# Tensor-product message passing on a graph: a bucket's 17 tiles cut into parts of 4, 6 and 7 instead of 5, 6 and 6

## The chip, the core and the metric

The kernel runs on one core of one Trainium2 chip. The metric is the device time of one execution in microseconds (us); lower is better. The core has five engines with an instruction queue each: PE (TensorE, the matmuls; PEld is its weight load), DVE (VectorE), ACT (ScalarE), POOL (GpSimd) and SP (SyncE). In this kernel SP issues the plain DMAs and POOL the indirect ones, in which a list of row numbers says what is read or written.

## What is computed

A graph has N = 10000 nodes and E = 640000 edges. Each node carries 64 channels of 4 components, 256 floats. Each edge has a source, a destination, four values Y and four features.

```python
R = silu(edge_feat @ w_rad)                      # (E, 64)
xs = x[src]                                      # (E, 64, 4), gathered
tp = jnp.einsum('eci,ef,ifo->eco', xs, Y, cg)    # (E, 64, 4)
msg = R[:, :, None] * tp
agg = segment_sum(msg.reshape(-1, 256), dst, N).reshape(N, 64, 4)
return jnp.einsum('ncm,cd->ndm', agg, w_mix)     # (N, 64, 4)
```

Sources and destinations are drawn at random. So each edge needs a row of x from an arbitrary place, and its message goes to an arbitrary node.

## The kernel before, in words

**The sort.** Edges are handled in tiles of 128, one edge to a partition. The kernel first sorts them by destination into buckets of NB = 32 nodes, of which there are 313; 18 buckets make a group, and there are 18 groups (the last one is short, with 7 buckets). The sort has two passes, and both work through chunks of 12 tiles. Pass 1 (`pass1`) packs an edge into 10 words and sends it to its group; pass 2 (`pass2`) reads a group back and sends its edges to their buckets. For one chunk `route` computes where each edge goes. VectorE spreads the words over slots (`spread`, lines 637 to 645: a mask, then X) and makes a part of the one-hot rows (`rows`, lines 654 to 660), ScalarE makes the others, PE permutes (`move`), ScalarE evicts (`evict`), and POOL stores the rows with one indirect DMA (`store`, line 687; grp is the table of pass 1, bkt that of pass 2). Each batch of chunks also needs `tables` of counts and offsets, a chain of small steps over PE, ScalarE and VectorE.

**The parts.** The edges are cut into three parts by SPLIT (line 39). Each entry has a share of the edges and the number of tiles that a bucket gets from this part, 5, 6 and 6 of BT = 17. Lines 103 to 106 turn the shares into ranges of tiles, rounded to 24. Line 111 gives the tiles of a group in each part: its mean number of edges with a margin, rounded up. A bucket that gets more edges from a part than it has room for passes the rest on to the later parts. In the last part two neighbouring buckets share one tile, so units there have 6 and 5 tiles in turn.

**The messages.** One unit is one bucket in one part (`messages`), so there are 3 x 313 = 939 units. `gather` fetches the unit's rows of x, one indirect DMA of POOL for each tile (line 1030), LG = 5 units ahead, into LG + 2 buffers named xg. `turn` transposes the features of the unit's tiles on PE, in two blocks of three tiles each, which overlap where a unit has five. `turned` copies them to SBUF on ScalarE, `radial` multiplies them with the radial weights on PE, and `silu` runs on ScalarE in place. `spots` builds the matrix S (destination and Y) on VectorE (lines 1066 and 1069; lines 1073 to 1077 for the shared tile), `products` multiplies xg with the radial scalars on VectorE (line 1083), and `sums` adds the tiles up in PSUM with two matmuls for each (line 1098). In the first two parts `evict` copies the sums out on ScalarE (line 1127) into the tile Gp, which has two buffers, and SP stores it to DRAM (line 1128). In the last part `fetch` reads the two stored sums back (line 1108, tile "old", three buffers), `evict` adds them on VectorE (lines 1123 and 1125), and `mix` applies cg and w_mix for four buckets at a time.

**The order of the work.** The first part's pass 1 runs alone, with the clearing of the tables woven in (lines 1549 to 1560). Then `groups` runs all else interleaved, in quarter steps of a unit. While the messages of one part run, pass 2 of the same part is worked off, each group in time for its messages, and pass 1 of the next part is spread evenly (`later`, lines 1189 to 1194, with due times and costs by the number of chunks). The messages of the last part have only its pass 2 beside them. The order of the instructions of PE, VectorE and ScalarE is exactly as the program writes it; on POOL and SP a scheduler orders them ahead of the run. Every engine works through its own queue in order.

Constants that VectorE reads often lie in a PSUM tile, dv: `v64` (the numbers 0 to 63), `i32` (its first 32 numbers), the work area `eq`, which has UT tiles' room, and a mask area, `vmsk`. `i128`, in SBUF, has the numbers 0 to 127.

Of the kernel before, what the change touches and what calls it, by code (L numbers as in the profile page):

```python
# [18 lines left out]
F = mybir.dt.float32  # L19
BF = mybir.dt.bfloat16  # L20
I32 = mybir.dt.int32
OP = mybir.AluOpType
AF = mybir.ActivationFunctionType
AX = mybir.AxisListType

P = 128
# [7 lines left out]
NB = 32  # L34
GN = B * NB
BT = 17
PT = 2 * BT - 1
UT = 6
SPLIT = ((0.32, 5), (0.37, 6), (0.31, 6))
LG = 5  # L40
LI = 8
HEAVY = 4
BIG = 16384.0
# [4 lines left out]
KR = 108  # L48
# [31 lines left out]
class Kernel:  # L80
    def __init__(self, ctx, tc, x, src, dst, Y, ef, w_rad, cg, w_mix, out):
# [16 lines left out]
        N, E, T, r = self.N, self.E, 12, 14  # L98
        assert N <= 127 << 7 and BT == sum(u for _, u in SPLIT) and B % 2 == 0 and HB % 2 == 0
        self.NG = (N + GN - 1) // GN  # L100
        assert self.NG <= B
        self.part, cut = [], 0
        for i, (share, _) in enumerate(SPLIT):
            end = cut + round(self.NT * share / (2 * T)) * 2 * T if i + 1 < len(SPLIT) else self.NT
            self.part.append((cut, end))
            cut = end
        self.gt = []
        for a, z in self.part:
# [8 lines left out]
        self.gbase = [[(k * NG + g) * self.p1.stride + self.p1.cap - self.gt[k][g] * P // r for g in range(NG)]  # L117
                      for k in range(len(SPLIT))]
        self.NBK = (N + NB - 1) // NB
# [6 lines left out]
        self.btile = [0]  # L126
        for _, u in SPLIT:
            self.btile.append(self.btile[-1] + u)

        self.p1.ovf = len(SPLIT) * NG * self.p1.stride  # L130
        self.p2.ovf = self.pairs * self.p2.stride
# [23 lines left out]
    def consts(self):  # L155
        nc, c = self.nc, self.cst
# [17 lines left out]
        self.i128 = iota("i128", [[1, P]])  # L174

        self.dv = self.ps.tile([P, 512], F, name="dv", tag="dv", bufs=1)
        self.v64 = self.dv[:, 0:P // 2]
        nc.vector.tensor_copy(self.v64, self.i128[:, :P // 2])
        self.i32 = self.dv[:, 0:NB]
        self.eq = self.dv[:, P:P + UT * NB].rearrange("p (t n) -> p t n", n=NB)  # L180
        self.vmsk = self.dv[:, P + UT * NB:]

        ib = self.ph.tile([P, P], BF, name="ib", bufs=1)
        nc.vector.tensor_copy(ib, self.i128)
        nc.vector.tensor_copy(self.dv[:, P // 2:P].bitcast(I32), ib.bitcast(I32))
        self.vb = self.dv[:, P // 2:P].bitcast(BF)

        self.sh = c.tile([P, 8], I32, name="sh")
        for a in range(2):
# [389 lines left out]
    def route(self, ps, quad, nt, table):  # L579
# [4 lines left out]
        nc, wk, tc, T, Q = self.nc, self.ph, self.tc, ps.T, 2  # L584
# [48 lines left out]
        def spread(c):  # L633
            _, slot, _ = MS[c // (2 * Q)]
            o, a = c % (2 * Q) * T, c % Q * T
            m = min(T, nt - c * T)
            msk = self.vmsk[:, :m * ps.r].rearrange("p (t s) -> p t s", s=ps.r)
            nc.vector.tensor_tensor(msk, self.v64[:, :ps.r].unsqueeze(1).to_broadcast([P, m, ps.r]),
                                    slot[:, o:o + m].unsqueeze(2).to_broadcast([P, m, ps.r]), op=OP.is_equal)
            X = self.ph.tile([P, self.xw], F, name="X", bufs=3)[:, :T * ps.rw].rearrange("p (t w) -> p t w", t=T)  # L640
            nc.vector.tensor_tensor(  # L641
                X[:, :m, :].rearrange("p t (s w) -> p t s w", w=W),
                msk.unsqueeze(3).to_broadcast([P, m, ps.r, W]),
                QD[c // Q][1][:, a:a + m, :].unsqueeze(2).to_broadcast([P, m, ps.r, W]), op=OP.mult)
            XO[c] = X
# [290 lines left out]
    def messages(self):  # L936

        nc, ph = self.nc, self.ph
        units = [((k, g), j) for k, g in self.segs for j in range(self.nb(g))]
        MT, FIN = max(u for _, u in SPLIT), len(SPLIT) - 1  # L940
        n = len(units)
        IDX, XG, PRE, ST_, RT, SS, VS, GP, GS, OLD, E9, ER, SX, VX = ({} for _ in range(14))
# [7 lines left out]
        def place(g, j):  # L950

            n = SPLIT[g[0]][1]
            if g[0] < FIN:
                return j * n, n
            return j // 2 * (2 * n - 1) + j % 2 * n, n - j % 2

        def tiles(k):
            return place(*units[k])

        def shared(k):  # L960

            g, j = units[k]
            return g[0] == FIN and j % 2 == 0 and j + 1 < self.nb(g[1])
# [60 lines left out]
        def gather(k):  # L1024
            g, j = units[k]
            si, (t0, ut) = IDX[g][0], tiles(k)
            xg = XG[k] = ph.tile([P, UT, 256], F, name="xg", bufs=LG + 2)
            for t in range(ut):
# [5 lines left out]
        def turn(k):  # L1034
            g, j = units[k]
            t0, ut = tiles(k)


            pre = PRE[k] = self.ps.tile([P, 512], F, name="pre", tag="pre", bufs=2)
            e = E9[g, j // HB].rearrange("p t h q k -> p (t h q k)")  # L1040
            b = t0 - place(g, j - j % HB)[0]
            for h, t in ((0, b), (1, b + ut - 3)):
                nc.tensor.matmul(pre[:KR, 256 + 128 * h:384 + 128 * h], e[:, 36 * t:36 * t + KR],  # L1043
                                 self.identb, start=True, stop=True)

        def turned(k):
            sT = ST_[k] = ph.tile([P, 2, P], BF, name="sT")
            nc.scalar.activation(sT[:KR].rearrange("p h e -> p (h e)"), PRE[k][:KR, 256:512], AF.Copy)  # L1048

        def radial(k):  # L1050
            ut = tiles(k)[1]
            R = RT[k] = PRE.pop(k)[:, :ut * 64]
            sT = ST_.pop(k)

            nc.tensor.matmul(R[:, :192], sT[:KR, 0], self.wr[:KR], start=True, stop=True)
            nc.tensor.matmul(R[:, 192:], sT[:KR, 1], self.wr[:KR, (6 - ut) * 64:], start=True, stop=True)  # L1056

        def silu(k):
            nc.scalar.activation(RT[k], RT[k], AF.Silu)  # L1059
# [1 line left out]
        def spots(k):  # L1061
            g, j = units[k]
            t0, ut = tiles(k)
            pb = self.pay[g][:, t0:t0 + ut]
            dl = IDX[g][1][:, t0:t0 + ut]
            nc.vector.tensor_tensor(self.eq[:, :ut], self.i32.unsqueeze(1).to_broadcast([P, ut, NB]),
                                    dl.unsqueeze(2).to_broadcast([P, ut, NB]), op=OP.is_equal)
            S = SS[k] = ph.tile([P, UT, NB, 4], F, name="S")
            nc.vector.tensor_tensor(S[:, :ut], self.eq[:, :ut].unsqueeze(3).to_broadcast([P, ut, NB, 4]),  # L1069
                                    pb[:, :, 1:5].unsqueeze(2).to_broadcast([P, ut, NB, 4]), op=OP.mult)  # L1070
            if shared(k):

                eq = ph.tile([P, NB], F, name="eqx", bufs=1)
                nc.vector.tensor_scalar(eq, self.v64[:, NB:2 * NB], dl[:, ut - 1:ut], None, op0=OP.is_equal)
                S = SX[k + 1] = ph.tile([P, NB, 4], F, name="Sx")
                nc.vector.tensor_tensor(S, eq.unsqueeze(2).to_broadcast([P, NB, 4]),
                                        pb[:, ut - 1, 1:5].unsqueeze(1).to_broadcast([P, NB, 4]), op=OP.mult)
# [25 lines left out]
        def fetch(k):  # L1103

            g, j = units[k]
            if g[0] == FIN:
                OLD[g, j] = ph.tile([P, FIN, 2, 4, NB], F, name="old", bufs=3)
                nc.sync.dma_start(OLD[g, j].rearrange("p a h f n -> p a (h f n)"),
                                  self.sums[g[1] * B + j].rearrange("a p q -> p a q"))

        def evict(k):
            g, j = units[k]
            final = g[0] == FIN
            if not final:
                to = ph.tile([P, 2, 4, NB], F, name="Gp")
            else:
                if j % 4 == 0:
                    GS[g, j // 4] = ph.tile([P, 2, 4, 4, NB], F, name="Gs")
                to = GS[g, j // 4][:, :, :, j % 4, :]
            G = GP.pop((g, j)).rearrange("p h n f -> p h f n")  # L1120
            if final:
                old = OLD.pop((g, j))
                nc.vector.tensor_tensor(to, old[:, 0], G, op=OP.add)
                for a in range(1, FIN):
                    nc.vector.tensor_tensor(to, to, old[:, a], op=OP.add)  # L1125
            else:
                nc.scalar.activation(to, G, AF.Copy)  # L1127
                nc.sync.dma_start(self.sums[g[1] * B + j, g[0]], to.rearrange("p h f n -> p (h f n)"))
# [18 lines left out]
        def mixed(k, po):  # L1147
# [6 lines left out]

        quarters = (((index, LI), (gather, LG), (fetch, 1), (turn, 2), (sums, 0), (silu, 1), (piece(0), 5), (piece(1), 4),
                     (piece(2), 3)), ((turned, 2), (spots, 1)),
# [85 lines left out]
    def mark(self):  # L1242
        for s in self.marks:
            self.nc.tensor.wait_ge(s, 1)

    def chunks(self, part):
        lo, hi = self.part[part]
        return (hi - lo + self.p1.T - 1) // self.p1.T
# [351 lines left out]
```

## Time and profile before

| | |
|---|---|
| median of 3 runs | 8426.91 us (8418.68 to 8428.72) |
| the profiled execution | 8430.4 us, of which the span from the first to the last instruction is 8428.6 us |
| mean granted TensorE clock | 0.855 |
| busy share of the span: DVE, PE, POOL, PEld, ACT | 85%, 71%, 70%, 59%, 55% |
| gathers of x by POOL (line 1030) | 5165, mean 957 ns, 4940.6 us in all |
| stores of the sort by POOL (line 687) | 417 to grp and 489 to bkt, mean 1008 ns |
| products (line 1083) | 939, mean 1615 ns |
| moved by DMA | 1051.54 MB |

How to read it: the shares are means over stages that differ much, so each stage is looked at by itself below. In the list of groups a line gives the program's line, the engine, the operation, output and inputs by the program's names, shapes and count, then the busy time in us and the mean of one in ns, and then the idle time of the engine just before them and what ended it. "issue" as that reason means that the engine waited for nothing that the profile shows. A lower-case q behind an engine's name is its sequencer, which issues and waits. The list of windows gives for each stretch its length, and for each engine its busy time and its number of instructions.

### The profile page before, as it was taken

To read this page: it belongs to the slowest core of one execution; us is meant where nothing else is said; L and a number is where in the kernel's file an instruction comes from. 1 tells how busy PE (TensorE), PEld (TensorE's weight loads), DVE (VectorE), ACT (ScalarE), POOL (GpSimd) and SP (SyncE) were. 2 spreads that over 40 slices of the span, in tenths; PEclk is the share of its full clock that TensorE was granted. 3 is DMA by queue.
4 is the path that set the end of the run, shared out by engine and by line. 5 is a ranking of instruction groups with operands and counts; after the bars stand their busy time and mean duration, and the time that the engine had idled before them with its cause. 6 is when DMAs were issued, how large, how long until landed. Compare 5 with 4: busy or idle time off the path is not lost. (4 is left out here: it accounts for less than half of the span.)

```text
span 8428.6 us, 133579 instructions
## 1 busy us (share of the span) xinstructions
PE 5985.1 (71%) x41164; PEld 4943.4 (59%) x41164; DVE 7181.2 (85%) x14990; ACT 4614.3 (55%) x12740; POOL 5881.9 (70%) x6113
## 2 busy tenths in 40 slices
PE   5666776777767767776676676766677777778776
PEld 3334655656555656565565565555566666666666
DVE  8988999999999889988898898867787888878775
ACT  5876666666666746655565565653443443434321
POOL 1226676777767767777777777777777777777776
PEclk8977888888888879888888888887898989888888
DMA  5313343443434434444444444444455555555543
GB/s 185 112 59 96 113 117 107 118 116 112 118 110 120 119 112 129 121 122 123 120 122 124 120 119 125 116 120 121 133 147 145 145 146 145 146 148 143 146 139 114
DMA packets 691501, 1051.54 MB, mean 125 GB/s; under 512 B 268789, under 2 KB 499107, under 8 KB 690792
## 3 DMA queue, kind: packets, MB, share of 16 engines
q0 software_dynamic: 285888, 732.64, 30.5%
q1 hardware_dynamic: 402312, 301.08, 12.1%
q10 hardware_dynamic: 2592, 9.19, 0.3%
q8 instruction: 345, 5.65, 0.3%
q14 instruction: 364, 2.98, 0.1%
HBM read 841.86 MB, written 215.89 MB: 125 GB/s over the span
## 5 line engine op out<-in xcount | busy, mean ns | idle before, releaser
L1030 POOL DMA_INDIRECT xg<-in_x_dram,sidx x5165 | 4940.6, 957 | 1750.4 <-issue 1345.0
L1098 PE MATMUL G<-S,xg 128*128 128x128 f32 x20660 | 2989.8, 310 | 158.2 <-ACT Gp L1127 129.4
L1098 PEld LDWEIGHTS G<-S,xg 128*128 128x128 f32 x20660 | 2837.7, 222 | 202.2 <-ACT Gp L1127 153.3
L675 PE MATMUL pr<-X,oh 128*128 128x300 bf16 (+1 forms) x10573 | 1668.3, 312 | 548.5 <-DVE oh L657 411.4
L1083 DVE TENSOR_TENSOR xg<-xg,pre 128x1536 f32<-128x1536 f32 (+1 forms) x939 | 1516.4, 1615 | 540.3 <-DMA xg<-in_x_dram,sidx 303.3
L665 ACT ACTIVATE sq<-i,rowf 128x128 f32<-128x128 f32 x6132 | 1882.1, 391 | 11.2 <-DVE rowf L626 7.3
L641 DVE TENSOR_TENSOR X<-dv,Wt 128x1800 f32<-128x1800 f32 (+4 forms) x906 | 1741.6, 1922 | 62.1 <-PE pr L675 10.4
L675 PEld LDWEIGHTS <-oh 128*128 128x128 bf16 x10573 | 1080.1, 105 | 983.1 <-DVE oh L657 483.7
L666 ACT ACTIVATE oh<-sq,ones 128x1024 bf16<-128x1024 f32 (+3 forms) x906 | 967.1, 1067 | 27.1
L1069 DVE TENSOR_TENSOR S<-dv,pay 128x768 f32<-128x768 f32 (+1 forms) x939 | 836.7, 891 | 87.3 <-PE G L1098 29.8
L1043 PE MATMUL pre<-identb,e 128*108 128x128 bf16 x1878 | 291.2, 241 | 867.5 <-DVE xg L1083 866.6
L1043 PEld LDWEIGHTS <-e 128*108 128x108 bf16 x1878 | 236.8, 140 | 1041.1 <-issue 792.3
L1059 ACT ACTIVATE pre<-pre 128x384 f32<-128x384 f32 (+1 forms) x939 | 426.6, 454 | 716.3 <-PE pre L1056 551.0
L687 POOL DMA_INDIRECT grp<-rt,idx x417 | 420.2, 1008 | 529.0 <-ACT rt L683 196.9
L1127 ACT ACTIVATE Gp<-G 128x256 f32<-128x256 f32 x626 | 238.6, 381 | 892.0 <-PE G L1098 647.3
L687 POOL DMA_INDIRECT bkt<-rt,idx x489 | 492.7, 1008 | 224.7 <-issue 112.4
L1048 ACT ACTIVATE sT<-pre 108x256 bf16<-108x256 f32 x939 | 353.2, 376 | 527.1 <-PE pre L1043 525.2
L1143 PE MATMUL po<-wf,Gs 128*128 128x256 f32 (+2 forms) x1392 | 390.8, 443 | 184.6 <-DVE Gs L1125 184.6
L683 ACT ACTIVATE rt<-pr 128x300 bf16<-128x300 f32 (+1 forms) x906 | 358.7, 396 | 278.6 <-PE pr L678 118.5
L1143 PEld LDWEIGHTS po<-wf,Gs 128*128 128x128 f32 (+2 forms) x1392 | 282.5, 209 | 278.1 <-DVE Gs L1125 181.7
L657 DVE TENSOR_TENSOR oh<-dv,pair 128x640 bf16<-128x640 bf16 (+2 forms) x869 | 420.6, 488 | 0.3
L609 ACT ACTIVATE pc<-pp 128x432 f32<-128x432 f32 (+3 forms) x471 | 236.3, 502 | 295.5 <-DVE pos L618 227.5
(286 smaller groups left out, 6086.1 us busy)
## 6 DMA issues: line engine op xcount, KB each, us to landing
xg<-in_x_dram,sidx POOLq DMA_INDIRECT x5165
sums<-Gp SPq DMA_DIRECT2D x626, 128.0 KB
old<-sums SPq DMA_DIRECT2D x313, 256.0 KB
bkt<-z SPq DMA_DIRECT2D x26, 990.0 KB
pay<-bkt SPq DMA_DIRECT2D x68, 225.0 KB
grp<-z SPq DMA_DIRECT2D x17, 590.0 KB
Wt<-grp SPq DMA_DIRECT2D x17, 590.0 KB
ye<-in_Y_dram SPq DMA_DIRECT2D x103, 96.0 KB
```

What stands on the lines that cost most here:

```text
L641: nc.vector.tensor_tensor(X[:, :m, :].rearrange("p t (s w) -> p t s w", w=W), msk.unsqueeze(3).to_broadcast([P, m, ps.r, W]), QD[c // Q][1 ...
L665: nc.scalar.activation(sq[:, u, :], self.i128, AF.Square, bias=to, scale=-1.0)
L666: nc.scalar.activation(oh[:, v:v + len(at), :], sq[:, :len(at), :], AF.Relu, bias=self.ones[:, 0:1], scale=-2.0)
L675: nc.tensor.matmul(pr[:, :2 * ps.rw], oh[:, u, :], X[:, u, :].bitcast(BF), start=(u == 0), stop=(not on and u == m - 1))
L687: st = nc.gpsimd.indirect_dma_start(out=ps.dst, out_offset=bass.IndirectOffsetOnAxis(ap=idx[:, i:i + 1], axis=0), in_=RT.pop(c), in_offset ...
L1030: nc.gpsimd.indirect_dma_start(out=xg[:, t, :], out_offset=None, in_=self.x, in_offset=bass.IndirectOffsetOnAxis(ap=si[:, u:u + 1], axis=0))
L1043: nc.tensor.matmul(pre[:KR, 256 + 128 * h:384 + 128 * h], e[:, 36 * t:36 * t + KR], self.identb, start=True, stop=True)
L1059: nc.scalar.activation(RT[k], RT[k], AF.Silu)
L1069: nc.vector.tensor_tensor(S[:, :ut], self.eq[:, :ut].unsqueeze(3).to_broadcast([P, ut, NB, 4]), pb[:, :, 1:5].unsqueeze(2).to_broadcast([P ...
L1083: nc.vector.tensor_tensor(V, V, R.unsqueeze(3).to_broadcast([P, ut, 64, 4]), op=OP.mult)
L1098: nc.tensor.matmul(G[:, h].rearrange("p n f -> p (n f)"), v[:, 32 * h:32 * h + 32, :].rearrange("p c i -> p (c i)"), s.rearrange("p n f -> ...
L1143: nc.tensor.matmul(po[:nn, :256], Gs[:, h, f].rearrange("p b n -> p (b n)")[:, :nn], self.wf[:, h, f, :], start=(h + f == 0), stop=(h + f ...
```

## The change

The shares become 0.258, 0.375 and 0.367, with 4, 6 and 7 tiles of a bucket; the sum stays 17. Units of the last part now have 7 and 6 tiles in turn. The transposes of a unit go in as many blocks of three tiles as it takes: two for 4, 5 or 6 tiles, three for 7, with the last block drawn back so that it ends with the unit's last tile. `turned` copies as many blocks as there are, and `radial` runs one matmul for each block, on the columns that no earlier block has covered.

Units have up to seven tiles (UT), so the buffers of xg and S grow. In return gathers go four units ahead (LG), with six xg buffers instead of seven; Gp has one buffer instead of two, and "old" has two (the pool's own number) instead of three. The PSUM tile dv is laid out anew: the 64 numbers of `v64` become the 32 of `i32`, and the shared tile's comparison (line 1074) takes its numbers 32 to 63 from `i128`.

```diff
-UT = 6
-SPLIT = ((0.32, 5), (0.37, 6), (0.31, 6))
-LG = 5
+UT = 7
+SPLIT = ((0.258, 4), (0.375, 6), (0.367, 7))
+LG = 4
...
-            msk ... self.v64[:, :ps.r] ...
+            msk ... self.i32[:, :ps.r] ...
...
-            for h, t in ((0, b), (1, b + ut - 3)):
-                nc.tensor.matmul(pre[:KR, 256 + 128 * h:384 + 128 * h], e[:, 36 * t:36 * t + KR],
+            for h, t in enumerate(self.thirds(ut)):
+                t += b
+                nc.tensor.matmul(pre[:KR, P + P * h:2 * P + P * h], e[:, 36 * t:36 * t + KR],
                                  self.identb, start=True, stop=True)
...
-            sT = ST_[k] = ph.tile([P, 2, P], BF, name="sT")
-            nc.scalar.activation(sT[:KR].rearrange("p h e -> p (h e)"), PRE[k][:KR, 256:512], AF.Copy)
+            sT = ST_[k] = ph.tile([P, 3, P], BF, name="sT")
+            n = P * len(self.thirds(tiles(k)[1]))
+            nc.scalar.activation(sT[:KR].rearrange("p h e -> p (h e)")[:, :n], PRE[k][:KR, P:P + n], AF.Copy)
...
-            nc.tensor.matmul(R[:, :192], sT[:KR, 0], self.wr[:KR], start=True, stop=True)
-            nc.tensor.matmul(R[:, 192:], sT[:KR, 1], self.wr[:KR, (6 - ut) * 64:], start=True, stop=True)
+            done = 0
+            for h, t in enumerate(self.thirds(ut)):
+                nc.tensor.matmul(R[:, done * 64:(t + 3) * 64], sT[:KR, h], self.wr[:KR, (done - t) * 64:], start=True, stop=True)
+                done = t + 3
...
-                nc.vector.tensor_scalar(eq, self.v64[:, NB:2 * NB], dl[:, ut - 1:ut], None, op0=OP.is_equal)
+                nc.vector.tensor_scalar(eq, self.i128[:, NB:2 * NB], dl[:, ut - 1:ut], None, op0=OP.is_equal)
...
-                OLD[g, j] = ph.tile([P, FIN, 2, 4, NB], F, name="old", bufs=3)
+                OLD[g, j] = ph.tile([P, FIN, 2, 4, NB], F, name="old")
...
-                to = ph.tile([P, 2, 4, NB], F, name="Gp")
+                to = ph.tile([P, 2, 4, NB], F, name="Gp", bufs=1)
...
+    @staticmethod
+    def thirds(n):
+        return [min(3 * h, n - 3) for h in range((n + 2) // 3)]
```

More of the change, by code (lines that the diff above doesn't have):

```diff
@@ L176, in consts @@
         self.dv = self.ps.tile([P, 512], F, name="dv", tag="dv", bufs=1)
-        self.v64 = self.dv[:, 0:P // 2]
-        nc.vector.tensor_copy(self.v64, self.i128[:, :P // 2])
         self.i32 = self.dv[:, 0:NB]
-        self.eq = self.dv[:, P:P + UT * NB].rearrange("p (t n) -> p t n", n=NB)
-        self.vmsk = self.dv[:, P + UT * NB:]
+        nc.vector.tensor_copy(self.i32, self.i128[:, :NB])
+        o = NB + P // 2
+        self.eq = self.dv[:, o:o + UT * NB].rearrange("p (t n) -> p t n", n=NB)
+        self.vmsk = self.dv[:, o + UT * NB:]
         ib = self.ph.tile([P, P], BF, name="ib", bufs=1)
         nc.vector.tensor_copy(ib, self.i128)
-        nc.vector.tensor_copy(self.dv[:, P // 2:P].bitcast(I32), ib.bitcast(I32))
-        self.vb = self.dv[:, P // 2:P].bitcast(BF)
+        nc.vector.tensor_copy(self.dv[:, NB:o].bitcast(I32), ib.bitcast(I32))
+        self.vb = self.dv[:, NB:o].bitcast(BF)
         self.sh = c.tile([P, 8], I32, name="sh")
@@ L637, in spread @@
             msk = self.vmsk[:, :m * ps.r].rearrange("p (t s) -> p t s", s=ps.r)
-            nc.vector.tensor_tensor(msk, self.v64[:, :ps.r].unsqueeze(1).to_broadcast([P, m, ps.r]),
+            nc.vector.tensor_tensor(msk, self.i32[:, :ps.r].unsqueeze(1).to_broadcast([P, m, ps.r]),
                                     slot[:, o:o + m].unsqueeze(2).to_broadcast([P, m, ps.r]), op=OP.is_equal)
```

## The prediction, made before the changed kernel was run

> **What bounds the kernel now.** I first cut the span where VectorE starts the products (L1083) of a part's first unit; 313 of them lie in each part (window, its length, VectorE's busy time on that line and its count, clock, DMA share, GB/s).
>
> ```profile
> 718.00:3301.90 2583.90, 463.34 (x313) 0.85 0.40 115
> 3301.90:6014.10 2712.20, 547.12 (x313) 0.84 0.42 122
> 6014.10:8428.60 2414.50, 505.93 (x313) 0.89 0.50 142
> ```
>
> Call these stages A, B and C, and what lies ahead of them the prelude. The same windows for whole engines:
>
> ```profile
> core 0: us, PE busy (x) PEld busy (x) DVE busy (x) ACT busy (x) POOL busy (x), PEclk, DMA share, GB/s
> 0.00:718.00 718.00, 417.42 (x2369) 245.21 (x2369) 646.45 (x1769) 521.05 (x1403) 188.93 (x204) 0.83 0.35 113
> 718.00:3301.90 2583.90, 1840.01 (x12782) 1511.60 (x12783) 2364.87 (x4979) 1655.56 (x4649) 1826.45 (x1891) 0.85 0.40 115
> 3301.90:6014.10 2712.20, 1886.01 (x13406) 1598.59 (x13404) 2291.56 (x4376) 1544.65 (x4255) 2059.57 (x2143) 0.84 0.42 122
> 6014.10:8428.60 2414.50, 1841.64 (x12609) 1587.97 (x12609) 1878.35 (x3870) 893.03 (x2435) 1806.96 (x1876) 0.89 0.50 142
> ```
>
> POOL looks 76% busy in B and 75% in C. Its groups in the middle of C, and windows inside the stages, say more:
>
> ```profile
> L1030 POOL DMA_INDIRECT xg<-in_x_dram,sidx x1378 | 1317.0, 956 | 419.8 <-issue 380.8 <-DMA xg<-in_x_dram,sidx 9.7 <-DVE Gs L1123 5.8
> L687 POOL DMA_INDIRECT bkt<-rt,idx x126 | 126.9, 1007 | 38.4 <-issue 34.1 <-ACT sq L665 2.1 <-ACT pre L1059 0.9
> ```
>
> ```profile
> 150.00:550.00 400.00, 256.01 (x1536) 154.00 (x1537) 396.17 (x918) 332.86 (x894) 103.83 (x104) 0.87 0.33 113
> 1500.00:2000.00 500.00, 364.54 (x2555) 299.59 (x2554) 466.43 (x966) 332.69 (x931) 360.36 (x373) 0.85 0.41 117
> 3400.00:5600.00 2200.00, 1534.74 (x10917) 1294.86 (x10917) 1893.34 (x3585) 1291.03 (x3555) 1671.12 (x1736) 0.84 0.42 121
> 6100.00:8000.00 1900.00, 1486.76 (x10178) 1269.38 (x10178) 1554.45 (x3308) 773.45 (x2116) 1442.14 (x1504) 0.90 0.51 146
> ```
>
> Nearly all of POOL's idle time is "issue", 0.3 us after each indirect DMA. 1900/1504 = 1.2633 us per POOL instruction; B has 2712.2/2143 = 1.266. So in B and C POOL never rests: a stage lasts as long as its count of indirect DMAs times 1.263. Stage A would need 1891 x 1.263 = 2389 us by that and takes 2584. There VectorE is the limit, 93% busy in 1500 to 2000, and in the prelude it is 99% busy (150 to 550). So: DVE bounds the prelude and A, POOL bounds B and C. Work moved from A to C leaves an engine that has nothing else to spare, and lands on another like it.
>
> **The prelude.** Counts of the sort's stores, first pass (rows to grp), by stage:
>
> ```profile
> 150.00:550.00 400.00, 103.83 (x104) 0.87 0.33 113
> 0.00:718.00 718.00, 134.83 (x134) 0.83 0.35 113
> 718.00:3301.90 2583.90, 166.45 (x165) 0.85 0.40 115
> 3301.90:6014.10 2712.20, 118.87 (x118) 0.84 0.42 122
> ```
>
> One chunk takes 400/104 = 3.85 us of a full VectorE. The parts hold 1608, 1848 and 1544 tiles of edges now; by lines 103 to 106 the new shares give 1296, 1872 and 1832, that is 108, 156 and 153 chunks of 12 for 134, 154 and 129. The 26 chunks that leave the prelude are worth 26 x 3.85 = 100 us. Line 111 then gives a full group of the first part 83 tiles for 103: 7 chunks of the second pass for 9, 122 in the part for 157. Ahead of A lie 17 of them (rows to bkt):
>
> ```profile
> 0.00:718.00 718.00, 16.69 (x17) 0.83 0.35 113
> ```
>
> Some four of those go (one of the short first group's, three of the next one's), about 12 us (an estimate from the chunk's VectorE rows below, 2.03 + 0.35 + 0.48 us; 0 to 20). With fewer steps to weave into, the last of SP's clears come in a bunch ahead of the next load; I take zero, 20 at most. Prelude: -112.
>
> **Stage A.** Per unit, 5 tiles become 4. By form, A's rows and then B's, where units have 6:
>
> ```profile
> L1083 DVE TENSOR_TENSOR xg<-xg,pre 128x1280 f32<-128x1280 f32 x313 | 463.3, 1480 | 49.6 <-ACT pre L1059 22.1 <-DMA xg<-in_x_dram,sidx 17.2 <-ACT e L1011 3.4
> ...
> L641 DVE TENSOR_TENSOR X<-dv,Wt 128x1800 f32<-128x1800 f32 x144 | 292.7, 2033 | 13.7 <-PE pr L675 1.8 <-PE pre L1056 0.5
> L1069 DVE TENSOR_TENSOR S<-dv,pay 128x640 f32<-128x640 f32 x313 | 258.1, 825 | 29.9 <-PE G L1098 6.8 <-DVE dv L1066 0.5
> L657 DVE TENSOR_TENSOR oh<-dv,pair 128x640 bf16<-128x640 bf16 x311 | 147.4, 481 | 0.0
> L1066 DVE TENSOR_TENSOR dv<-dv,dlc 128x160 f32<-128x160 f32 x312 | 103.8, 333 | 5.7
> ...
> L638 DVE TENSOR_TENSOR dv<-dv,slot 128x180 f32<-128x180 f32 x144 | 50.7, 352 | 2.2
> ...
> L641 DVE TENSOR_TENSOR X<-dv,Wt 128x1050 f32<-128x1050 f32 x16 | 20.0, 1252 | 1.5
> ...
> L638 DVE TENSOR_TENSOR dv<-dv,slot 128x105 f32<-128x105 f32 x16 | 4.4, 273 | 0.5
> ```
>
> ```profile
> L1083 DVE TENSOR_TENSOR xg<-xg,pre 128x1536 f32<-128x1536 f32 x313 | 547.1, 1748 | 229.7 <-ACT pre L1059 123.9 <-DMA xg<-in_x_dram,sidx 82.5 <-issue 13.0
> ...
> L1069 DVE TENSOR_TENSOR S<-dv,pay 128x768 f32<-128x768 f32 x313 | 299.7, 957 | 45.8 <-PE G L1098 22.3 <-DVE dv L1066 0.5
> ...
> L1066 DVE TENSOR_TENSOR dv<-dv,dlc 128x192 f32<-128x192 f32 x313 | 113.9, 364 | 5.9
> ```
>
> A tile costs 268 + 132 + 31 = 431 ns of VectorE, so 313 x 0.431 = 135 us go. The second pass has 20 tiles and two chunks less in a group. A tile costs (2033 - 1252)/5 = 156 ns in X, (352 - 273)/5 = 16 in the mask and as much again in the position step (an estimate from the mask): 3.8 us for 20. Six fewer one-hot tiles on VectorE (481/5 = 96 ns each) make 0.6. The fixed parts of two chunks make some 1.3 (an estimate: eight instructions at the 1252 - 7 x 156 = 160 ns that X's row leaves). Together 5.7 us, for 15.5 groups (31 of the 35 chunks) 90 us. The 17.2 us of waits for gathers go, as POOL is then no longer close. Against that, A takes four more first-pass chunks (156 for 154, and more of the third part's 153 begin in A): +15. A: -135 - 90 - 17 + 15 = -227, to 2357, give or take 30. POOL needs 1891 - 313 - 31 + 4 = 1551 instructions, 1959 us: it will idle where it hardly did.
>
> **Stage B.** Its units keep six tiles and its groups ten chunks. It takes 140 first-pass chunks for 118 and one second-pass chunk more: 23 x 1.263 = +29, if VectorE keeps under the 93% of stage A. In 3400 to 5600 it has 1893/2200 = 86%; 22 x 3.85 = 85 us more over 2228 make 89%. So POOL still bounds it, with less air than before.
>
> **Stage C.** Units of 7 and 6 tiles for 6 and 5: 313 more gathers. Full groups of 117 tiles for 99: ten chunks for nine, 17 more stores. 330 x 1.263 = +417. VectorE has room (1554/1900 = 82%), and its fixed costs per unit stay. The third block of transposes, for the 157 units of seven tiles:
>
> ```profile
> L1043 PE MATMUL pre<-identb,e 128*108 128x128 bf16 x1878 | 291.2, 241 | 867.5 <-DVE xg L1083 866.6
> L1048 ACT ACTIVATE sT<-pre 108x256 bf16<-108x256 f32 x939 | 353.2, 376 | 527.1 <-PE pre L1043 525.2
> ```
>
> One transpose and one radial matmul more, about 0.5 us of PE (the second priced like the first), 157 times 75 us on an engine at 78%, and half of 376 ns of ScalarE (773/1900 = 41% busy): beside POOL's work, nothing. Were PE the bound there, it would be those 75.
>
> **Buffers.** Gathers run four units ahead in six buffers, not five in seven. In C that is 26 tiles for 27.5, in B 24 for 30: no price while POOL is the slow end. The queues matter more. SP issues the store of each unit's sums, and ScalarE's copy (L1127) needs the buffer that this store empties; behind that copy on ScalarE stand the silu and the copies of later units, and VectorE's products wait for those. ScalarE's waits in B, SP's, and one such event on ScalarE's timeline (start, length, in brackets the idle time before):
>
> ```profile
> ACT Gp L1127 <- DMA sums<-Gp: 217.5, 16, 26.3
> ...
> ACT rt L683 <- DMA bkt<-rt,idx: 40.8, 8, 13.0
> ```
>
> ```profile
> SPq L919 <- DMA bkt<-rt,idx: 292.2, 15, 36.1
> SPq L856 <- DMA grp<-rt,idx: 129.8, 8, 37.2
> ```
>
> ```profile
> 4739.31 0.37 ACT L1127 ACTIVATE Gp<-G 128x256 f32<-128x256 f32 x1
> ...
> 4744.65 0.38 ACT L1127 ACTIVATE Gp<-G 128x256 f32<-128x256 f32 x1 [1.59 <-PE G L1098]
> ...
> 4773.10 0.38 ACT L1127 ACTIVATE Gp<-G 128x256 f32<-128x256 f32 x1 [26.35 <-DMA sums<-Gp]
> ```
>
> Once per group SP stands at a load that waits for a sort store, and that store queues on POOL behind gathers already issued. With one buffer ScalarE stops a unit sooner (4744.65 - 4739.31 = 5.3 us); with gathers one unit less ahead, the store comes a unit (six gathers, 7.6 us) sooner. I take zero; the ends are -16 x 7.6 = -122 us of ScalarE waits and +95 (18 groups x 5.3). Neither reaches POOL while it has units in hand: it lost nothing to today's 217.5. "old" with two buffers leaves its load two units (2 x 2831/313 = 18 us), about SP's mean stand of 292/15 = 19: zero, or 18 us where the longest, 36.1, recurs.
>
> The new eqx reads its ramp from SBUF, not PSUM:
>
> ```profile
> L1074 DVE TENSOR_SCALAR eqx<-dv,dlc x156: 240/241/244, 6013.4 to 8364.4; 128x32 f32<-128x32 f32 x156
> ```
>
> At most 156 x 0.241 = 38 us of VectorE, which is not C's bound; I take zero. The Trainium skill, "SBUF — State Buffer", section "Who interferes with whom", says that a VectorE tensor_scalar whose operands all lie in SBUF can take the port pair that GpSimd needs for its descriptors, and hold it for the whole instruction. That speaks against this line of the change, and no row here tests it for this line; it is the fourth rival.
>
> **Sum.** -112 - 227 + 29 + 417 = +107. The profiled execution's own time was 8430.4 us (span 8428.6), so 8537; the median of the runs, 8426.9, is 3.5 lower, so I say 8534, 1.3% slower.
>
> **Rivals.**
> 1. Faster: VectorE closes its gaps in A. Of A's 2584 us it idles 219, and once POOL stops being close, nothing but VectorE's own order may be left. At the prelude's density A would take (2365 - 227)/0.99 = 2160, and the whole 8534 - 197 = 8337. Break-even is A at 2250. For it: POOL's 95% in A. Against: the waits for gathers there are only 17.2 us. Chance 0.09.
> 2. Slower still: stage B turns into a chain of ScalarE stalls, as the single sums buffer meets a VectorE without air to catch up. All 95 us then show: 8629. It decides if POOL runs out of free xg buffers in such a stall. Against: POOL loses nothing today. The Trainium skill ("Trainium Kernel Development and Optimization", "Best Practices") asks for two buffers to overlap transfer and compute. Chance 0.14.
> 3. No difference, within 0.2%: half of the first case, A near 2250, 8430. Chance 0.04.
> 4. The port: each eqx stops POOL for its length in C, where POOL is the bound: 38 more, 8572. Chance 0.06.
>
> **Numbers.** Forecast 0.67, own range 8485 to 8585. Range 8460 to 8630: it leaves out rivals 1 and 3, and little else. 0.2% is about what a measurement of this kernel can tell from no change. Faster 0.09, same 0.04, slower 0.87.
>
> **What would show it.** Right: the first L1083 near 606; 313 products to about 2963; B with POOL at 1.263 per instruction and some 2166 of them; C 2206 instructions in about 2830 us. POOL gaps other than "issue" should appear in A alone. Wrong: A below 2250; C's count times 1.263 not its time; POOL waiting for PE G in B; or ScalarE waits on sums<-Gp far over 217 with POOL idle beside them.

## The result and the profile after

The changed kernel takes 8526.81 us (median of 4 runs, 8523.28 to 8528.30), the kernel before 8425.35 us (median of 4, 8418.68 to 8428.72). The ratio is 1.0121, 95% interval 1.0103 to 1.0138: slower by 1.2%. The profiled execution after has a span of 8525.4 us. Only two of the experiments, plain_c2 and plain_a2, ran on chips where the kernel before takes this time; on the chips of all the others it takes 10.1 to 10.2 ms in every run, and their numbers stand beside the kernel before of their own chip.

The windows of the whole engines, cut as before where the first product (now L1087) of a part starts, with the count of the products below:

```profile
core 0: us, PE busy (x) PEld busy (x) DVE busy (x) ACT busy (x) POOL busy (x), PEclk, DMA share, GB/s
0.00:600.50 600.50, 326.63 (x1923) 193.98 (x1924) 530.98 (x1512) 419.49 (x1135) 151.26 (x163) 0.85 0.38 126
600.50:2940.80 2340.30, 1631.88 (x11191) 1330.18 (x11191) 2144.07 (x4864) 1522.39 (x4373) 1508.91 (x1558) 0.84 0.37 108
2940.80:5724.40 2783.60, 1959.27 (x13792) 1653.13 (x13792) 2401.96 (x4607) 1630.59 (x4479) 2115.34 (x2192) 0.84 0.42 121
5724.40:8525.40 2801.00, 2096.28 (x14496) 1845.00 (x14495) 2102.16 (x3931) 1031.35 (x2661) 2103.31 (x2184) 0.86 0.48 138
```

```profile
600.50:2940.80 2340.30, 379.63 (x313) 0.84 0.37 108
2940.80:5724.40 2783.60, 546.96 (x313) 0.84 0.42 121
5724.40:8525.40 2801.00, 589.63 (x313) 0.86 0.48 138
```

| | before | after | measured | predicted |
|---|---|---|---|---|
| prelude | 718.0 | 600.5 | -117.5 | -112 |
| stage A | 2583.9 | 2340.3 | -243.6 | -227 |
| stage B | 2712.2 | 2783.6 | +71.4 | +29 |
| stage C | 2414.5 | 2801.0 | +386.5 | +417 |
| span | 8428.6 | 8525.4 | +96.8 | +107 |

The first two stages give back 361 us and the last two take 458. POOL's groups in the middle of C, and the same inner windows as before:

```profile
L1030 POOL DMA_INDIRECT xg<-in_x_dram,sidx x1384 | 1325.0, 957 | 421.9 <-issue 377.5 <-DMA bkt<-rt,idx 15.5 <-DMA xg<-in_x_dram,sidx 7.3
L687 POOL DMA_INDIRECT bkt<-rt,idx x118 | 118.5, 1004 | 36.0 <-issue 24.7 <-ACT oh L666 2.7 <-ACT rt L683 2.4
```

```profile
1500.00:2000.00 500.00, 351.28 (x2424) 286.85 (x2422) 466.29 (x1059) 335.00 (x960) 325.49 (x336) 0.85 0.37 108
3100.00:5300.00 2200.00, 1573.27 (x11117) 1320.49 (x11116) 1958.89 (x3718) 1348.99 (x3703) 1672.24 (x1731) 0.85 0.42 121
6100.00:8000.00 1900.00, 1447.68 (x9995) 1268.60 (x9994) 1490.16 (x2878) 762.71 (x1981) 1442.39 (x1502) 0.86 0.49 140
```

In C POOL issues one indirect DMA each 1900/1502 = 1.265 us, as before, and there are more of them. In A VectorE is as full as before (466 of 500 us), while POOL fell from 373 to 336 instructions in the same 500 us. POOL's waits say the same, first in A, then in B (us in all, times, longest):

```profile
POOL xg L1030 <- issue: 312.1, 1023, 0.5
POOL xg L1030 <- PE G L1102: 205.5, 79, 7.7
```

```profile
POOL xg L1030 <- issue: 467.3, 1533, 0.3
...
POOL xg L1030 <- DMA xg<-in_x_dram,sidx: 12.6, 40, 0.7
```

In A, POOL now waits 205 us until `sums` (PE G) has read a buffer that a gather is to fill (118 us before). In B the longest wait of any gather is 0.7 us, in the second row; in all other rows it is 0.3 us, which is the gap between any two indirect DMAs.

### The profile page after: what moved, and what is told of

Read it like the earlier page. It is cut to its first block, busy times and chain, and to the rows that moved or that the text cites. A ratio compares the mean times of both kernels' runs of the same rounds, so it can differ in the third digit from the quotient of the medians.

```text
span 8525.4 us, 133668 instructions
## 1 busy us (share of the span) xinstructions
PE 6014.1 (71%) x41402; PEld 5022.3 (59%) x41402; DVE 7179.2 (84%) x14912; ACT 4603.8 (54%) x12645; POOL 5878.8 (69%) x6095
## 5 line engine op out<-in xcount | busy, mean ns | idle before, releaser
L1030 POOL DMA_INDIRECT xg<-in_x_dram,sidx x5165 | 4952.5, 959 | 1883.8 <-issue 1333.9
L1102 PE MATMUL G<-S,xg 128*128 128x128 f32 x20660 | 3077.3, 316 | 152.7 <-ACT Gp L1131 130.3
L1087 DVE TENSOR_TENSOR xg<-xg,pre 128x1536 f32<-128x1536 f32 (+2 forms) x939 | 1516.2, 1615 | 625.0 <-DMA xg<-in_x_dram,sidx 441.9
L641 DVE TENSOR_TENSOR X<-dv,Wt 128x1800 f32<-128x1800 f32 (+2 forms) x888 | 1736.1, 1955 | 65.6 <-PE pr L675 14.9
L666 ACT ACTIVATE oh<-sq,ones 128x896 bf16<-128x896 f32 (+3 forms) x888 | 956.6, 1077 | 26.7
L1073 DVE TENSOR_TENSOR S<-dv,pay 128x768 f32<-128x768 f32 (+2 forms) x939 | 836.9, 891 | 79.3 <-PE G L1102 21.1
L1063 ACT ACTIVATE pre<-pre 128x384 f32<-128x384 f32 (+2 forms) x939 | 425.6, 453 | 808.1 <-PE pre L1059 623.5
L1050 ACT ACTIVATE sT<-pre 108x256 bf16<-108x256 f32 (+1 forms) x939 | 370.5, 395 | 584.4 <-PE pre L1044 582.8
L683 ACT ACTIVATE rt<-pr 128x280 bf16<-128x280 f32 (+1 forms) x888 | 351.9, 397 | 281.2 <-PE pr L678 156.4
L1011 ACT ACTIVATE e<-er 128x192 bf16<-128x192 f32 (+6 forms) x522 | 205.1, 393 | 495.3 <-DVE er L1021 480.8
L657 DVE TENSOR_TENSOR oh<-dv,pair 128x640 bf16<-128x640 bf16 (+3 forms) x887 | 424.1, 483 | 0.5
```

The source lines that it names most:

```text
L641: nc.vector.tensor_tensor(X[:, :m, :].rearrange("p t (s w) -> p t s w", w=W), msk.unsqueeze(3).to_broadcast([P, m, ps.r, W]), QD[c // Q][1 ...
L666: nc.scalar.activation(oh[:, v:v + len(at), :], sq[:, :len(at), :], AF.Relu, bias=self.ones[:, 0:1], scale=-2.0)
L1030: nc.gpsimd.indirect_dma_start(out=xg[:, t, :], out_offset=None, in_=self.x, in_offset=bass.IndirectOffsetOnAxis(ap=si[:, u:u + 1], axis=0))
L1087: nc.vector.tensor_tensor(V, V, R.unsqueeze(3).to_broadcast([P, ut, 64, 4]), op=OP.mult)
L1102: nc.tensor.matmul(G[:, h].rearrange("p n f -> p (n f)"), v[:, 32 * h:32 * h + 32, :].rearrange("p c i -> p (c i)"), s.rearrange("p n f -> ...
```

## The experiments

**Less work for POOL, one stage at a time.** Three kernels take one gather from every unit of one part. A plain DMA on SP's queue brings the first 128 rows of x in its place, so the messages of these edges are computed from wrong rows. The edit is the same but for the part's number:

```diff
             for t in range(ut):
                 u = t0 + t
+                if g[0] == 2 and t == 0:
+                    nc.sync.dma_start(xg[:, t, :], self.x[:P, :])
+                    continue
                 nc.gpsimd.indirect_dma_start(
```

For stage C:

> The kernel of plain_c once more, on a chip where the kernel before takes 8425 us: the first tile of each unit of the last part by a plain DMA of the first 128 rows of x on SP's queue, wrong rows for these edges. Theory (POOL bounds C and VectorE has room): the full 313 x 1.263 = 395 us less than the changed kernel, 8132 us within 30, C near 2406. Rival (VectorE's chain, the two buffers of the old sums or PE bound C): less than half of it.

Measured: 8141.22 us (2 runs) beside 8428.91 for the kernel before, ratio 0.9661 (0.9633 to 0.9689). That is 386 us under the changed kernel's 8526.81. The window of C:

```profile
5717.20:8133.50 2416.30, 1979.95 (x14495) 1750.52 (x14495) 2101.24 (x3931) 1028.92 (x2660) 1803.66 (x1876) 0.93 0.56 160
```

POOL has 1876 instructions instead of 2184 and C takes 2416 us instead of 2801: 385/308 = 1.25 us for each that is gone. The kernel before has the same 1876 in its C and takes 2414.5 us for them. VectorE and PE have the same work as in the changed kernel and do it in 385 us less (PE at a granted clock of 0.93, not 0.86), and the DMA engines move as much (160 GB/s in the shorter time, 138 in the longer). So POOL bounds C, and the rival falls: neither VectorE's chain, nor the two buffers of the old sums, nor the third block of transposes holds C up.

For stage A:

> The kernel of plain_a once more, on such a chip: the same in the first part's units. Theory (VectorE bounds stage A): no change, 8527 us within 20, stage A near 2340. Rival (POOL or the gathers' lead bounds A too): up to 395 us less.

Measured: 8513.32 us (2 runs), ratio 1.0102 (1.0073 to 1.0132), 13 us under the changed kernel, whose interval (1.0103 to 1.0138) overlaps with this one. The window of A, and POOL's waits in it:

```profile
599.30:2930.30 2331.00, 1626.61 (x11193) 1322.90 (x11193) 2140.34 (x4864) 1522.85 (x4374) 1216.61 (x1251) 0.84 0.38 108
```

```profile
POOL xg L1033 <- PE G L1105: 411.9, 131, 12.6
```

307 instructions less, and A is 9 us shorter. POOL spends the time that it saves waiting: its wait for free buffers doubled, from 205.5 to 411.9 us. The same edit is worth 385 us in one stage and 9 in another. POOL does not bound A.

For stage B the kernel ran three times, each time on a chip where the kernel before takes 10.1 to 10.2 ms, and so did the first runs for A and C. What was on record for B, the first time (the two later runs had the same theory on record):

> The same in the second part's units: 313 indirect DMAs less on POOL in stage B, wrong rows for these edges. Theory (POOL bounds B, with VectorE close behind): B falls from 2784 us only until VectorE is as full as in A, 2402 us of work at 91.6 to 93% busy, 2575 to 2620: 165 to 210 us less in all, 8320 to 8360. If POOL alone counted: 395 less, 8132. If stalls of ScalarE on the sums' store bounded B: no change.

Measured: 10101.28, 10109.30 and 9969.41 us, ratios 0.9886 (0.9865 to 0.9907), 0.9881 (0.9858 to 0.9903) and 0.9862 (0.9814 to 0.9911). How far VectorE stands behind POOL in B was thus not measured on a chip of the kind that the prediction spoke of; it stays open. The runs of A and C on these chips had this on record:

> The changed kernel, with the first tile of each unit of the first part filled by a plain DMA of the first 128 rows of x on SP's queue instead of POOL's gather: 313 indirect DMAs less on POOL in stage A, and the messages of these edges are computed from wrong rows. Everything else is the same. Theory (VectorE bounds stage A): no change, 8527 us within 20, stage A near 2340. Rival (POOL or the gathers' lead bounds A too): up to 313 x 1.263 = 395 us less.

> The same in the last part's units: 313 indirect DMAs less on POOL in stage C, wrong rows for these edges. Theory (POOL bounds C and VectorE has room): the full 313 x 1.263 = 395 us less, 8132 us within 30, C near 2406. Rival (VectorE's chain, the two buffers of the old sums or PE bound C): less than half of it.

They gave 1.0021 (1.0005 to 1.0037) and 0.9951 (0.9934 to 0.9968) of 10221.14 us. There the theory's numbers do not hold; the last section shows what these chips do.

**The old parts with the new buffers.** The changed kernel with one line put back:

```diff
-SPLIT = ((0.258, 4), (0.375, 6), (0.367, 7))
+SPLIT = ((0.32, 5), (0.37, 6), (0.31, 6))
```

> The changed kernel with the old shares and tiles (5, 6, 6), but with its other edits kept: gathers four units ahead in six buffers, one buffer for the stored sums, two for the old sums, the new layout of the constants. Theory (the parts alone cost the time: VectorE bounds the prelude and stage A, POOL stages B and C): the time of the kernel before, 8425 us, within 15. Rival (fewer buffers and a shorter lead cost): up to 95 us more, 8520, with POOL idle in stage B beside ScalarE waits for the store of the sums.

Measured: 1.0011 (1.0000 to 1.0023) of 10221.14 us. Once more:

> The kernel of split_back once more, on such a chip: the changed kernel with the old shares and tiles (5, 6, 6) but its other edits kept (lead of four units, six xg buffers, one buffer for the stored sums, two for the old sums, constants' layout). Theory (the parts alone cost the time): the time of the kernel before, 8425 us, within 15. Rival (fewer buffers and a shorter lead cost): up to 95 us more, 8520, with POOL idle in stage B beside ScalarE waits for the store of the sums.

Measured: 1.0006 (0.9996 to 1.0015) of 10227.34 us. The lead, the buffers and the constants' layout cost 0.1% there, 0.2% at the upper ends of the intervals. POOL is not full on these chips, so the runs do not test the buffers under a full POOL. For that there is only the trace after, where ScalarE's wait in B for the store of the sums is

```profile
ACT Gp L1131 <- DMA sums<-Gp: 130.8, 13, 26.3
```

It was 217.5 us before, with two buffers. In the same stage SP waits less at the loads that need POOL's stores:

```profile
SPq L856 <- DMA grp<-rt,idx: 117.6, 8, 33.6
SPq L919 <- DMA bkt<-rt,idx: 88.0, 10, 27.6
```

L919 alone had 292.2. That the shorter lead is the reason, as the prediction had it, fits these rows but is not shown: no run on a chip where the kernel before takes 8425 us changes the lead or the buffers alone.

**More and less one-hot work for VectorE.** Three kernels change how many of a chunk's 12 one-hot tiles ScalarE makes. The first is the changed kernel:

```diff
-            self.p1.act = self.p2.act = 7
+            self.p1.act = self.p2.act = 5
```

> The changed kernel, but ScalarE makes 5 of the 12 one-hot tiles of a chunk instead of 7 once the messages have begun, so VectorE makes two more, 2 x 96 ns a chunk. Theory (VectorE bounds A alone): A has 298 chunks, so it grows by 57 us; B (313 chunks, 60 us) and C (158, 30 us) hide them under POOL: 8584 us in all, 15 more at most where B's VectorE is dense. Rival (A is bound by waits between the engines or by POOL): no change or a gain, as ScalarE is relieved. If VectorE bounded everything: 148 us more.

Measured: 10444.13 us, ratio to the kernel before 1.0210 (1.0193 to 1.0227), on a chip where that one takes 10227.34. The other two start from the kernel before, with the shares 0.31, 0.37, 0.32 and 10 or 9 in place of 7:

> The kernel before with two edits that follow from the theory: shares 0.31, 0.37, 0.32 for the tiles 5, 6, 6 (the first part's pass 1 has 130 chunks instead of 134, its groups 100 tiles instead of 103), and ScalarE makes 10 of the 12 one-hot tiles of a chunk once the messages have begun, not 7. Theory: prelude 4 x 3.85 = 15 us less; A 324 chunks x 3 x 96 ns = 93 less and 10 less for the smaller groups, still above POOL's 2389; B 5 more for four more stores; 8425 - 113 = 8312 us. Rival (ScalarE, 64% busy in A before and some 78% with this, becomes late for the silu): half of that gain or none.

> The kernel before with two edits that follow from the theory: shares 0.31, 0.37, 0.32 for the tiles 5, 6, 6 (the first part's pass 1 has 130 chunks instead of 134, its groups 100 tiles instead of 103), and ScalarE makes 9 of the 12 one-hot tiles of a chunk once the messages have begun, not 7. Theory: prelude 4 x 3.85 = 15 us less; A 324 chunks x 2 x 96 ns = 62 less and 10 less for the smaller groups; B 5 more for four more stores; 8425 - 82 = 8343 us. Rival (A is bound by the chain between the engines, and ScalarE becomes late for the silu): no gain or a loss.

Measured: 1.0192 (1.0171 to 1.0213) of 10227.34 us and 1.0109 (1.0073 to 1.0146) of 10112.17 us. They were to test VectorE's part in A and to beat both kernels. On these chips both lose; how much of that is ScalarE's extra work and how much the other shares is not separated. None of the three was run on a chip where the kernel before takes 8425 us, so what was expected of them stays untested, and a better version was not found.

## Why the prediction was right

**Time and sign.** 8534 us was forecast and 8526.81 measured; the sum of four terms was +107 and came out +96.8. The terms themselves were off by -5.5, -16.6, +42.4 and -30.5 us; that the sum is so close is in part luck, as they cancel.

**The prelude** (-112, measured -117.5). Stores to grp by stage, and stores to bkt ahead of A:

```profile
0.00:600.50 600.50, 111.57 (x108) 0.85 0.38 126
600.50:2940.80 2340.30, 173.50 (x171) 0.84 0.37 108
2940.80:5724.40 2783.60, 139.38 (x138) 0.84 0.42 121
```

```profile
0.00:600.50 600.50, 12.79 (x13) 0.85 0.38 126
```

26 first-pass chunks less, and four second-pass chunks less, as worked out. The counts 171 and 138 stand against 169 and 140: two more chunks of the third part than assumed fell into A.

**Stage A** (-227, measured -243.6). The per-tile price by form:

```profile
L1087 DVE TENSOR_TENSOR xg<-xg,pre 128x1024 f32<-128x1024 f32 x313 | 379.6, 1213 | 48.0 <-ACT pre L1063 39.1 <-DMA xg<-in_x_dram,sidx 5.7 <-PE prep L415 1.5
...
L1073 DVE TENSOR_TENSOR S<-dv,pay 128x512 f32<-128x512 f32 x313 | 216.4, 692 | 31.8 <-PE G L1102 7.8 <-DVE dv L1070 0.5
...
L1070 DVE TENSOR_TENSOR dv<-dv,dlc 128x128 f32<-128x128 f32 x312 | 92.3, 296 | 5.4
```

(1480 - 1213) + (825 - 692) + (333 - 296) = 437 ns a tile, for 431; over 313 units that is 137 us. VectorE's busy time fell by 2364.9 - 2144.1 = 221 us, so the sort's work in A fell by 84 (the forecast was 90 - 15 = 75). The rest of the 244 is idle time, 219 to 196 us; of the 17.2 us of waits for gathers, which were to go, 5.7 stayed. VectorE idles 8.4% of A and idled 8.5%: it stayed as dense as it was. That is the fall of rival 1, which needed A below 2250. (Its 2160 counted the 17 us of waits as VectorE's work; without them it is (2365 - 210)/0.99 = 2177.) VectorE's longest waits in A:

```profile
DVE xg L1087 <- ACT pre L1063: 39.1, 23, 4.9
DVE sts L535 <- PE ddp L523: 9.3, 7, 3.3
DVE S L1073 <- PE G L1102: 7.8, 8, 2.2
```

All of its waits that the profile gives a reason for add up to some 86 us in A (101 before), 3.7% of the stage. For the other 110 us of idle time it gives none; they are 23 ns in the mean for each of 4864 instructions. If these stay, A takes some 2254 us even without any wait (an estimate from this trace). That POOL does not bound A is shown by plain_a2; that VectorE does rests on this agreement, on its share and on how little it waits. Adding to VectorE's work was tried only on the chips where the kernel before takes 10.2 ms.

**Stages B and C** (+29 and +417, measured +71.4 and +386.5). Their sum is 458 for 446; the counts are 2192 + 2184 = 4376 POOL instructions for 2166 + 2206 = 4372. The split was off, not the sum. The gathers (L1030) in B and C after the change, and in C before it:

```profile
2940.80:5724.40 2783.60, 1800.27 (x1879) 0.84 0.42 121
5724.40:8525.40 2801.00, 1920.45 (x2002) 0.86 0.48 138
```

```profile
6014.10:8428.60 2414.50, 1637.63 (x1708) 0.89 0.50 142
```

C has 2002 of the last part's 2035 gathers in its window, so 33 were out before its first product; before the change it was 1722 - 1708 = 14. At the end of B POOL is further ahead of VectorE, and 19 gathers, 24 us, moved from C's account to B's. The forecast for B had taken no change in that lead. The rest of the 42 us by which B was missed is seven more instructions (five gathers and two stores), 9 us, and 10 us in the spacing (2783.6/2192 = 1.270 us for 1.266).

**The third block of transposes** was priced at nothing beside POOL, and plain_c2 shows it: with POOL relieved, the same PE work fits into 2416 us.

**Buffers.** Zero as a net price fits the trace: POOL loses nothing in B to ScalarE's waits for the sums' store. How the shorter lead and the single buffer share in that is not shown. For "old" the working said 0 to 18 us; the wait came out larger, and stays hidden because POOL is the slow end. VectorE's waits in C:

```profile
DVE xg L1087 <- DMA xg<-in_x_dram,sidx: 336.9, 92, 6.9
...
DVE Gs L1127 <- DMA old<-sums: 101.3, 14, 8.1
```

In plain_c2, where VectorE has less time to spare, the same wait is 4.8 us:

```profile
DVE Gs L1130 <- DMA old<-sums: 4.8, 8, 1.4
```

**Rival 2** (stalls of ScalarE in B) falls: 130.8 us of waits, and no gap of POOL in B above 0.7 us. **Rival 4** (the port) falls by the spacing in C, 1.2650 for 1.2633 us: 1.7 ns for 2184 instructions are 4 us, not 38 (and the difference is two instructions in 1900 us). The new eqx itself:

```profile
L1078 DVE TENSOR_SCALAR eqx<-i,dlc x156: 229/232/477, 5698.9 to 8462.6; 128x32 f32<-128x32 f32 x156
```

Its median is 9 ns shorter than the 241 of the form that read PSUM, but its longest is nearly twice that form's 244, and its mean is 262 ns for 241, 3 us in all. The rule of the Trainium skill ("SBUF — State Buffer", "Who interferes with whom") fits that tail, if here VectorE is the one that waits now and then; POOL's spacing shows no price.

## What to carry to other kernels

Cut the span into stages and ask in each which engine's work equals its length: work that leaves a stage is worth its price on that stage's bound, and work that arrives costs its price on the other one's. Here a unit's tile was worth 0.44 us of VectorE where it left and 1.26 us of POOL where it came in; with the sort's work that moved along, the first two stages gave back 361 us and the last two took 458. A busy share of 75% can be a full engine, as POOL's was here with 0.3 us behind each DMA: count instructions per us, not busy time, where each is followed by a fixed gap. And to prove a bound, take the same work from one engine in each stage in turn: 385 us here and 9 us there says more than any share.

## What the runs showed of the hardware that was not expected

On some chips the same kernel takes 10.1 to 10.2 ms, in every run, and the reason could not be settled; whether it lies in these chips or in the time of the runs is not separated either. POOL's and VectorE's instructions take what they take elsewhere (a gather 956 ns, a product 1615 ns); a matmul of `sums` takes 325 ns in the mean for 310. The prelude, where POOL gathers little, is nearly as fast as elsewhere. The kernel with the old parts (split_back2), by the same four stages:

```profile
0.00:731.60 731.60, 420.35 (x2370) 247.49 (x2371) 647.57 (x1770) 521.69 (x1403) 183.92 (x199) 0.81 0.33 110
731.60:3737.80 3006.20, 1997.37 (x12782) 1597.06 (x12783) 2363.41 (x4977) 1659.95 (x4649) 1823.88 (x1890) 0.79 0.34 99
3737.80:7034.00 3296.20, 2110.26 (x13406) 1720.68 (x13403) 2299.96 (x4377) 1551.11 (x4257) 2083.07 (x2167) 0.79 0.35 101
7034.00:10235.30 3201.30, 2052.24 (x12609) 1735.06 (x12609) 1888.05 (x3870) 891.54 (x2432) 1788.65 (x1857) 0.80 0.38 106
```

Against 718, 2584, 2712 and 2414 us that is 2%, 16%, 22% and 33% more, at a granted clock of 0.79 to 0.80 for 0.84 to 0.89. POOL's count fills only 2345 of C's 3201 us, and VectorE is 59% busy: none of them is full. What grew are waits that end by something the profile cannot name ("remote"), on ScalarE above all and on VectorE and POOL too, and "issue" ahead of PE's matmuls. The trace before shows no "remote" wait, and 30 us of such "issue" in all:

```profile
ACT rt L683 <- remote: 700.1, 85, 26.3
ACT pre L1063 <- remote: 626.1, 113, 19.0
ACT Gp L1131 <- remote: 625.8, 151, 11.2
```

```profile
PE G L1102 <- issue: 404.9, 387, 8.2
...
PE pr L675 <- issue: 316.9, 353, 9.7
```

On such chips 37 us more of VectorE's work in A add little or nothing: A takes 2602 us, beside 2591 and 2603 in two kernels that have the changed kernel's A. The A of act5, then that of plain_c:

```profile
617.00:3219.40 2602.40, 1723.55 (x11194) 1385.42 (x11194) 2187.58 (x4864) 1294.80 (x3772) 1505.59 (x1558) 0.81 0.34 97
```

```profile
617.70:3208.90 2591.20, 1747.20 (x11195) 1398.95 (x11195) 2150.39 (x4864) 1525.17 (x4376) 1506.86 (x1558) 0.80 0.34 97
```

Gathers cost there in every stage, though POOL has idle time in each: plain_a's A takes 2417.2 us (2591 to 2603 in the others), plain_b's B 3020.8 (3352 to 3377), plain_c's C 3570.0 (3833 to 3846):

```profile
609.90:3027.10 2417.20, 1665.51 (x11195) 1348.86 (x11195) 2144.73 (x4865) 1526.31 (x4376) 1217.36 (x1251) 0.84 0.36 104
```

```profile
3222.40:6243.20 3020.80, 2089.94 (x13793) 1730.13 (x13792) 2402.50 (x4608) 1634.28 (x4478) 1822.57 (x1885) 0.82 0.39 112
```

```profile
6585.60:10155.60 3570.00, 2236.05 (x14493) 1908.73 (x14492) 2107.35 (x3932) 1016.53 (x2649) 1797.88 (x1873) 0.79 0.38 108
```

That is 0.6 to 1.1 us for each gather gone. The granted clock rose in these stages too (0.84 for 0.80 to 0.81 in A), and its part is not separated. So neither of the two bounds of this document holds on them. A loop between PE and ScalarE that the gathers lengthen would fit all of this, but that is only argued; what slows such a chip stays open. The change's own price there can be put together from stages that the edits left alone: 618 + 2603 + 3352 + 3833 = 10406 us (the prelude of plain_c, A of plain_b, B and C of plain_a), beside 10247 for split_back on the same chip, 1.6% more.
